# Three steps instead of two per converted weight slot, and a reordered opening, in a fused attention and two-FFN kernel

## The chip, the cores and the metric

The kernel runs on one core of one Trainium2 chip. The metric is the device time of one execution in microseconds (us), the median over several runs.

## What is computed

The reference chains three things; the shapes are those of the run.

- Causal attention over q, k, v of shape (2, 12, 448, 64): softmax(q k^T / 8 with a causal mask) v, reshaped to 896 tokens by 768.
- A dense FFN: `h = x @ w_in` (768 by 2048), `g = h * sigmoid(1.702 h)`, `x = g @ w_out` (2048 by 768).
- A second, routed FFN: of 8 experts each token goes to the one with the largest gate logit; `relu(x @ w1[e]) @ w2[e]` (768 by 1024, 1024 by 768), scaled by the gate's probability and a sigmoid of a second gate.

The weights of the dense FFN, w_in and w_out, arrive as 64-bit floats (the launch views them as int64), all else as 32-bit.

## The kernel before, in words

The program is written under a manual schedule: each engine executes its instructions in the order in which the Python code emits them, and waits only for the semaphores of the data it needs. So the order of emission is the order of each queue.

**Attention.** The 24 heads are worked in 12 pairs. Each pair has seven blocks of 64 queries (both heads stacked to 128 rows), taken in the order JO, so the stage is 84 numbered steps, s = 0 to 83, plus a drain of six. A step emits, in this order: the transposes of the probabilities of the step four earlier (`p_tr`, L405, and the copies L408 or L410), the scores and mask products of this step (`qk`, L374 and L375), the normalisation of the step before (`norm`, L395 to L397, the last mostly on POOL), at some steps the transposes of the next pair's q and k (`tr_qk`, L356, with the copies L361 and L365) and the products with v (`av`, L423), then this step's maximum and exponential (`soft`, L386 and L388), and last, at s % 7 equal to 3 or 6 from s = 7 on, one `pump`.

**Slot conversion.** [...] A `Stream` turns each 512 KB piece (128 by 512 numbers) into a slot: a high part in PE's rounded float format and a low part, the rest. There are 48 pieces: 24 of w_in, 8 of w_out's last 256 columns (`oB`), 16 of its first 512 (`oA`). The generator `work` (L222) does one piece, and `pump(n)` advances it by n steps, a step being what lies up to the next `yield`. Step A has two DVE operations (L226 and L228) and then `st.flush()`, which emits the DVE subtraction L235 of the piece before; step B has one DVE operation (L232) and the ACT copy L234, and registers this piece's subtraction as `late`. Then the generator ends, the piece counts as ready, its raw buffer is given back and the next load is emitted on SP's queue (L218). A piece takes two steps. `need(key)` forces steps until a piece is ready. Nineteen slots (ring A) and five raw buffers exist; where no slot is free, a pump does nothing.

**First layer.** 16 blocks f of 128 hidden units, six pieces kk each; `l1_mm` (L444) emits six products per kk into two PSUM tiles, of 512 and 384 columns. Even f take their two tiles from a pool of three (`sc`), odd f from a pool of four (`tp`). After each kk of f = 0 to 11 there is one step of the pump, after each kk of f = 12 to 14 there are two; at the last block of each group of four a slot is freed after each kk. Then the block's sigmoid (ACT, L547) and product (DVE, L548) run in four pieces and free the tiles.

**Second layer.** For t = 0 to 6, first part B (256 columns), then part A (512): 16 kk with three products each (L587). Its left factor is split by `gsplit` (ACT L516, DVE L519, four per t), up to four ahead. `y` is copied by ACT (L609), sent out, transposed (L627) and used for the gate (L639). Pump rates per kk are R2 in part B (0.1 to 0.3) and R3, 1.2, in part A. When the last piece is done, the loads of the experts' weights begin (`fill`).

**Experts.** Blocks of 128 tokens per expert, whose weights stream in, are split (L307 on ACT, L308 on DVE) and used (L897).

**Opening.** POOL makes the identity; DVE copies it to bf16 (L171) and clears `wz` (L456); eight warming products on `wz` run on PE (L459) into an unused tile; `load_pair(0)` issues q's two and k's two transfers on SP's queue (L339), and v's and the next pair's follow there. `tr_qk(0, "q")` transposes q, ACT scales it in two halves (L361), `tr_qk(0, "k")` follows with one ACT copy (L365), and the first scores can start.

Of the kernel before, what the change touches and what calls it, by code (L numbers as in the profile page):

```python
# [9 lines left out]
F32 = mybir.dt.float32  # L10
F32R = mybir.dt.float32r
BF16 = mybir.dt.bfloat16
# [3 lines left out]
AF = mybir.ActivationFunctionType  # L16
ALU = mybir.AluOpType
# [98 lines left out]
def kernel(ctx, tc, q, k, v, w_in, w_out, w_gate, w_og, w1, w2, out):  # L116
    nc = tc.nc
# [4 lines left out]
    CP = 112  # L122
# [33 lines left out]
    def pool(name, side="left", **kw):  # L156
        return tc.tile_pool(name=name, bufs=1, side=side, reuse_waits="tile", **kw)

    def opened(p):
        es = ExitStack()  # L160
        return es, es.enter_context(p)
# [4 lines left out]
    with tc.manual_schedule():  # L166

        ident = const.tile([128, 128], F32, name="ident")
        make_identity(nc, ident)
        identb = const.tile([128, 128], BF16, name="identb")  # L170
        nc.vector.tensor_copy(identb, ident)  # L171
        cmask = const.tile([128, QB], BF16, name="cmask")
        for h in range(2):
            make_causal_mask(nc, cmask[QB * h:QB * h + QB], mask_val=NEG)
# [35 lines left out]
        def raw_tile(where, shape, dt):  # L210
            if where == "raw":
                return raws.tile(shape, dt, name="raw", tag="raw", bufs=RAW)
            return ringA.tile(shape, dt, name="rawA", tag=f"slotA{where}")

        def add64(keys, src, two=False, ring="A"):
            def load(where):
                raw = raw_tile(where, [128, 512], I64)
                nc.sync.dma_start(raw.rearrange("p (a n) -> p a n", a=2) if two else raw, src)  # L218
                return raw

            def work(keys, raw):
                slot = st.slots[keys[0]] = ring_slot(keys[0])  # L222
                r = raw.bitcast(U32).rearrange("p (n two) -> p n two", two=2)
                w = raws.tile([128, 512], F32, name="w32", tag="w32", bufs=2)
                wu = w.bitcast(U32)
                nc.vector.tensor_scalar(wu, r[:, :, 1], 3, 0x3FFFFFF8,  # L226
                                        op0=ALU.logical_shift_left, op1=ALU.bitwise_and)
                nc.vector.scalar_tensor_tensor(wu, r[:, :, 1], 0xC0000000, wu,  # L228
                                               op0=ALU.bitwise_and, op1=ALU.bitwise_or)
                st.flush()  # L230
                yield
                nc.vector.scalar_tensor_tensor(wu, r[:, :, 0], 29, wu,  # L232
                                               op0=ALU.logical_shift_right, op1=ALU.bitwise_or)
                nc.scalar.copy(slot[:, 0], w)  # L234
                st.late = keys[0], lambda: nc.vector.tensor_sub(slot[:, 1], w, slot[:, 0].bitcast(F32))  # L235

            st.add(keys, ring, load, work)
# [3 lines left out]
        def ring_slot(key):  # L241
            ring, place = st.home[key]
            if ring == "A":
                return ringA.tile([128, 2, 512], F32R, name="slotA", tag=f"slotA{place}")
            return xr_p[0].tile([128, 2, 512], F32R, name="slotX", tag=f"slotX{place}")
# [69 lines left out]
        es_a, ap_ = opened(pool("attn", side="right"))  # L315
# [4 lines left out]
        NQ = S // QB  # L320
        KC = 128
        NKC = -(-S // KC)
        ld = {}
        qkT = {}
        P_t = {}
# [7 lines left out]
        def load_pair(i):  # L333
            b, hp = pairs[i]
            r = {}
            for nm, src in (("q", q), ("k", k)):
                t = ap_.tile([CP, NB, 2, D], F32, name=nm + "raw", tag=nm + "raw", bufs=2)
                for h in range(2):
                    nc.sync.dma_start(t[:, :, h, :], src[b, 2 * hp + h].rearrange("(c p) d -> p c d", p=CP))  # L339
                r[nm] = t  # L340
            ld.setdefault(i, {}).update(r)

        def load_v(i):
            b, hp = pairs[i]
            t = ap_.tile([KC, 2, NKC, D], F32, name="vraw", tag="vraw", bufs=3)
            full = S // KC
            for h in range(2):
                nc.sync.dma_start(t[:, h, 0:full], v[b, 2 * hp + h, 0:full * KC].rearrange("(c p) d -> p c d", p=KC))
            nc.sync.dma_start(t[0:S - full * KC, :, full], v[b, 2 * hp:2 * hp + 2, full * KC:S].rearrange("h p d -> p h d"))
            ld.setdefault(i, {})["v"] = t  # L350

        def tr_qk(i, nm):
            src = ld[i][nm]
            ps = pa.tile([128, 512], F32, name="ps_tr", tag="tp", bufs=TP)[:, 0:S].rearrange("p (c n) -> p c n", c=NB)
            for c in range(NB):
                nc.tensor.transpose(ps[:, c], src[:, c].rearrange("p h d -> p (h d)"), ident[:CP, :CP])  # L356
            if nm == "q":
                dst = qz[i % 2]
                for h in range(2):
                    r = slice(64 * h, 64 * h + 64)  # L360
                    nc.scalar.mul(dst[r, :, h], ps[r].rearrange("d c p -> d (c p)").rearrange("d (j p) -> d j p", j=NQ),  # L361
                                  0.125)
            else:
                dst = ap_.tile([128, S], F32, name="kT", tag="kT", bufs=2)
                nc.scalar.copy(dst.rearrange("d (c p) -> d c p", c=NB), ps)  # L365
            qkT[i, nm] = dst
# [32 lines left out]
        def p_tr(i, j):  # L399
            if j == JO[0]:  # L400
                pT[i] = ap_.tile([KC, 2, NQ + 5 * (NKC - 1), QB], F32, name="pT", tag="pT", bufs=2)
            nch = j // 2 + 1
# [11 lines left out]
        def av(i, c):  # L414
            b, hp = pairs[i]
            if c == 0:
                po[i] = pa.tile([128, S], F32, name="ps_o", tag="o", bufs=1)
            ps = po[i]
            vt = ld[i]["v"]
            t = pT[i]  # L420
            kn = min(KC, S - c * KC)
            for h in range(2):
                nc.tensor.matmul(ps[64 * h:64 * h + 64, c * KC:S], vt[:kn, h, c, :],  # L423
                                 t[:kn, h, 7 * c:5 * c + NQ], start=c == 0, stop=c == NKC - 1)
            if c < NKC - 1:
                return
            del ld[i], pT[i], po[i]
            dst = xhi[:, hp, b * S:(b + 1) * S]
            nc.scalar.copy(dst, ps)
            nc.vector.tensor_sub(xlo[:, hp, b * S:(b + 1) * S], ps, dst.bitcast(F32))  # L430
# [16 lines left out]
        early = 0  # L447
        steps = [(i, j) for i in range(NP) for j in JO]
        load_pair(0)
        load_v(0)  # L450
        load_pair(1)
        nc.gpsimd.memset(qz[0], 0.0)
        load_v(1)
        load_v(2)
        wz = ap_.tile([128, 512], BF16, name="wz")
        nc.vector.memset(wz, 0.0)  # L456
        wps = pa.tile([128, 512], F32, name="ps_w", tag="o", bufs=1)
        for i in range(WARM):
            nc.tensor.matmul(wps, wz[:, 0:128], wz, start=True, stop=True)  # L459
        tr_qk(0, "q")  # L460
        for j in range(0, NQ, 2):
            nc.gpsimd.memset(Pb[j][:, QB * (j + 1):], 0.0)
        nc.gpsimd.memset(qz[1], 0.0)
        tr_qk(0, "k")
        for s in range(len(steps) + LAG + AV_AT[-1]):
            if 0 <= s - LAG < len(steps):
                p_tr(*steps[s - LAG])
            if s < len(steps):
                i, j = steps[s]
                if s % NQ == 0 and i + 2 < NP:  # L470
                    load_pair(i + 2)
                qk(i, j)
            if 1 <= s <= len(steps):
                norm(*steps[s - 1])
            for c in "kq":
                if s < len(steps) and i + 1 < NP and s % NQ == TR_AT[c]:
                    tr_qk(i + 1, c)
            for c in range(NKC):
                u = s - LAG - (NQ - 1) - AV_AT[c]
                if u >= 0 and u % NQ == 0 and u // NQ < NP:  # L480
                    av(u // NQ, c)
                    if c == NKC - 1 and u // NQ + 3 < NP:
                        load_v(u // NQ + 3)
            soft()
            if s >= len(steps) + L1_PAST and early < KD - 1:
                l1_mm(0, early)
                early += 1
            if s % NQ in PUMP_AT and s >= PUMP_FROM and s < len(steps) + PUMP_PAST:
                st.pump(1)
# [70 lines left out]
        ps = ctx.enter_context(pool("ps", space=PSUM))  # L560
# [477 lines left out]
```

## Time and profile before

| what | value |
|---|---|
| median of three runs | 625.28 us (625.07 to 625.89) |
| the profiled execution: its own time | 625.63 us |
| span in the profile | 623.5 us |
| mean granted PE clock | 0.987 |
| PE busy | 590.3 us, 95% of the span |
| DVE busy | 463.9 us, 74% |
| ACT busy | 376.9 us, 60% |
| POOL busy | 106.7 us, 17% |

The profiled execution took 625.63 us, of which the span, from the first to the last recorded instruction, is 623.5 us; 2.1 us lie around it. An engine's busy time is the sum over its instructions. PE's products are pipelined and their ends are modelled, so a busy PE is not a PE at its peak. PEld is PE's weight load, which overlaps the products. By the timeline, attention lasts until about 125 us, the first layer until 252 us, part B of the second until about 302 us, part A until about 389 us, and the experts take the rest.

### The profile page before, as it was taken

The numbers are of one execution on the slowest core, as the hardware profiler recorded it, in microseconds if no ns is written. First come the engines' busy times: TensorE is split into PE (matmuls) and PEld (weight loads), VectorE is DVE, ScalarE is ACT, GpSimd is POOL, SyncE is SP. The second block draws the span as 40 slices with busy tenths as digits, with TensorE's granted clock in tenths as the row PEclk, the third lists the DMA queues.
The fourth block names the chain that finished last, engine by engine and source line by source line (L and its number), as shares of the span: only waits on it lengthen the run. The fifth ranks groups of instructions, "written<-read, shape, count | busy, mean of one in ns | idle before, by whom it ended". The sixth has DMA issues, their size and how long they took to land. (4 is left out here: it accounts for less than half of the span.)

```text
span 623.5 us, 10060 instructions
## 1 busy us (share of the span) xinstructions
PE 590.3 (95%) x3326; PEld 473.6 (76%) x3326; DVE 463.9 (74%) x942; ACT 376.9 (60%) x743; POOL 106.7 (17%) x225
## 2 busy tenths in 40 slices
PE   7999999899979999889999999989999999999995
PEld 4665665578868888879877777767888888888884
DVE  2788888757858483797633447789998898889886
ACT  4878878623232323455433234678888888888885
POOL 3333333310000000000001002231631111001110
PEclk8999999999979999999999999999999999999998
DMA  5856554216434241433571503359999999999940
GB/s 134 245 125 141 123 126 116 56 57 184 142 111 115 89 136 37 143 116 119 176 263 38 150 17 119 111 183 347 349 368 353 318 383 377 380 381 378 383 161 20
DMA packets 93146, 118.02 MB, mean 189 GB/s; under 512 B 40208, under 2 KB 53408, under 8 KB 93090
## 3 DMA queue, kind: packets, MB, share of 16 engines
q1 hardware_dynamic: 88562, 109.05, 54.7%
q0 software_dynamic: 2512, 5.54, 2.5%
q10 hardware_dynamic: 2016, 2.75, 1.2%
q8 instruction: 28, 0.46, 0.4%
q14 instruction: 28, 0.23, 0.1%
HBM read 114.10 MB, written 7.54 MB: 195 GB/s over the span
## 5 line engine op out<-in xcount | busy, mean ns | idle before, releaser
L587 PE MATMUL py<-slotA,gs 128*128 128x256 f32 (+1 forms) x609 | 112.5, 337 | 1.0 <-DVE gs L519 1.0
L444 PE MATMUL ph<-xhi,slotA 128*128 128x512 f32 (+1 forms) x384 | 97.7, 374 | 5.6 <-DVE g L548 5.6
L587 PEld LDWEIGHTS py<-slotA,gs 128*128 128x128 f32 x609 | 90.8, 190 | 13.6 <-issue 2.6
L444 PEld LDWEIGHTS ph<-xhi,slotA 128*128 128x128 f32 x384 | 70.8, 191 | 16.5 <-issue 6.1
L234 ACT CAST slotA<-w 128x512 fp32r<-128x512 f32 x45 | 27.9, 621 | 63.1 <-DVE w L232 61.4
L308 DVE TENSOR_TENSOR ent<-wraw,ent 128x1024 fp32r<-128x1024 f32 x48 | 57.9, 1221 | 5.8 <-ACT ent L307 5.8
L444 PE MATMUL ph<-xlo,slotA 128*128 128x512 f32 x192 | 56.1, 373 | 0.0
L374 PE MATMUL sc<-kT,qz 128*128 128x64 f32 (+6 forms) x168 | 53.2, 401 | 2.8 <-ACT kT L365 2.4
L388 ACT ACTIVATE P<-sc,nmax 128x64 f32<-128x64 f32 (+6 forms) x84 | 40.3, 479 | 24.5 <-DVE nmax L386 14.7
L548 DVE TENSOR_TENSOR g<-ph,g 128x256 f32<-128x256 f32 x64 | 23.6, 389 | 41.5 <-ACT g L547 41.5
L897 PE MATMUL ps_h<-ent,xh 128*128 128x512 f32 x192 | 54.0, 402 | 0.0
L307 ACT CAST ent<-wraw 128x1024 fp32r<-128x1024 f32 x48 | 49.9, 1053 | 0.0
L519 DVE TENSOR_TENSOR gs<-g,gs 128x512 fp32r<-128x512 f32 x56 | 37.5, 683 | 16.6 <-ACT gs L516 16.6
L397 POOL TENSOR_SCALAR P<-P,rc 128x64 f32<-128x64 f32 (+2 forms) x72 | 36.0, 500 | 69.6 <-DVE rc L396 43.5
L516 ACT CAST gs<-g 128x512 fp32r<-128x512 f32 x56 | 33.8, 618 | 16.3 <-PE py L587 10.6
L386 DVE TENSOR_REDUCE nmax<-sc 128x1 f32<-128x64 f32 (+6 forms) x84 | 34.4, 411 | 10.7 <-PE sc L375 10.7
L547 ACT ACTIVATE g<-ph 128x256 f32<-128x256 f32 x64 | 20.9, 355 | 33.5 <-PE ph L444 17.2
L897 PEld LDWEIGHTS ps_h<-ent,xh 128*128 128x128 f32 x192 | 35.0, 188 | 7.6 <-DVE ent L308 0.3
L308 DVE TENSOR_TENSOR ent<-wrb,ent 128x1024 fp32r<-128x1024 f32 x30 | 36.3, 1223 | 4.7 <-ACT ent L307 4.2
L444 PEld LDWEIGHTS ph<-xlo,slotA 128*128 128x128 f32 x192 | 35.8, 192 | 4.6
L405 PE MATMUL ps_pT<-ident,P 128*128 128x128 f32 x192 | 37.8, 289 | 1.1
L228 DVE SCALAR_TENSOR_TENSOR w<-raw,w 128x512 uint32<-128x512 uint32 x46 | 35.0, 762 | 1.6
(189 smaller groups left out, 1175.5 us busy)
## 6 DMA issues: line engine op xcount, KB each, us to landing
wraw<-in_moe_w_dram SPq DMA_DIRECT2D x66, 512.0 KB
wrb<-in_moe_w_dram SPq DMA_DIRECT2D x48, 512.0 KB
wr<-in_moe_w_dram SPq DMA_DIRECT2D x30, 512.0 KB
raw<-in_moe_w_in_dram SPq DMA_DIRECT2D x24, 512.0 KB
raw<-in_moe_w_out_dram SPq DMA_DIRECT2D x22, 512.0 KB
qraw<-in_q_dram SPq DMA_DIRECT2D x24, 112.0 KB
kraw<-in_k_dram SPq DMA_DIRECT2D x24, 112.0 KB
vraw<-in_v_dram SPq DMA_DIRECT2D x24, 96.0 KB
```

The lines of the kernel that those rows point to most:

```text
L228: nc.vector.scalar_tensor_tensor(wu, r[:, :, 1], 0xC0000000, wu, op0=ALU.bitwise_and, op1=ALU.bitwise_or)
L307: nc.scalar.copy(hi, raw)
L308: nc.vector.tensor_sub(lo, raw, hi.bitcast(F32))
L374: nc.tensor.matmul(sc[:, :n], qT[:, j].rearrange("d h p -> d (h p)"), kT[:, :n], start=True, stop=False)
L386: nc.vector.tensor_reduce(nm, sc[:, :n], axis=AX.X, op=ALU.max, negate=True)
L388: nc.scalar.activation(Pb[j][:, :n], sc[:, :n], AF.Exp, bias=nm, scale=1.0, accum_out=sm)
L397: eng[NORM_ENG[j]].tensor_scalar(Pb[j][:, :n], Pb[j][:, :n], rc, 1.0, op0=ALU.mult, op1=ALU.mult)
L405: nc.tensor.transpose(ps[:, c].rearrange("p h q -> p (h q)"), Pb[j][:, c * KC:(c + 1) * KC], ident)
L444: nc.tensor.matmul(p[:, 0:128 * nt], wt, xt[:, kk, 128 * t0:128 * (t0 + nt)], start=kk == 0 and n == 0, stop=kk == KD - 1 and n == 2)
L519: glate.append(lambda: nc.vector.tensor_sub(gs[:, 1], src, gs[:, 0].bitcast(F32)))
L587: nc.tensor.matmul(py[:, :n], gt[:, kk % 4], wt, start=kk == 0 and m == 0, stop=kk == KF - 1 and m == 2)
L897: nc.tensor.matmul(hps[hf], xh[:, k0 + n], wt[:, n], start=k0 + n == 0 and m == 0, stop=False)
```

## The change

The slot conversion gets a second `yield`, after the ACT copy L234, so a piece takes three steps: A, B, and a third, C, that emits no arithmetic and only registers the subtraction and ends the piece (with the release of the raw buffer and the next load). The numbers of pumps and their rates stay as they are. In the opening, `wz` is cleared ahead of the identity's bf16 copy, a one-column exponential on ACT is put ahead of the first loads, the first pair's k is issued on ACT's queue, and the second half of the first pair's q is scaled by DVE.

```diff
--- before.py
+++ after.py
@@ -168,7 +168,6 @@
         ident = const.tile([128, 128], F32, name="ident")
         make_identity(nc, ident)
         identb = const.tile([128, 128], BF16, name="identb")
-        nc.vector.tensor_copy(identb, ident)
         cmask = const.tile([128, QB], BF16, name="cmask")
         for h in range(2):
             make_causal_mask(nc, cmask[QB * h:QB * h + QB], mask_val=NEG)
@@ -232,6 +231,7 @@
                 nc.vector.scalar_tensor_tensor(wu, r[:, :, 0], 29, wu,
                                                op0=ALU.logical_shift_right, op1=ALU.bitwise_or)
                 nc.scalar.copy(slot[:, 0], w)
+                yield
                 st.late = keys[0], lambda: nc.vector.tensor_sub(slot[:, 1], w, slot[:, 0].bitcast(F32))
 
             st.add(keys, ring, load, work)
@@ -320,6 +320,11 @@
         NQ = S // QB
         KC = 128
         NKC = -(-S // KC)
+        wz = ap_.tile([128, 512], BF16, name="wz")
+        nc.vector.memset(wz, 0.0)
+        ez = ap_.tile([128, 1], F32, name="ez")
+        nc.scalar.activation(ez, wz[:, 0:1], AF.Exp)
+        nc.vector.tensor_copy(identb, ident)
         ld = {}
         qkT = {}
         P_t = {}
@@ -334,9 +339,10 @@
             b, hp = pairs[i]
             r = {}
             for nm, src in (("q", q), ("k", k)):
+                dma = nc.scalar if i == 0 and nm == "k" else nc.sync
                 t = ap_.tile([CP, NB, 2, D], F32, name=nm + "raw", tag=nm + "raw", bufs=2)
                 for h in range(2):
-                    nc.sync.dma_start(t[:, :, h, :], src[b, 2 * hp + h].rearrange("(c p) d -> p c d", p=CP))
+                    dma.dma_start(t[:, :, h, :], src[b, 2 * hp + h].rearrange("(c p) d -> p c d", p=CP))
                 r[nm] = t
             ld.setdefault(i, {}).update(r)
 
@@ -358,8 +364,11 @@
                 dst = qz[i % 2]
                 for h in range(2):
                     r = slice(64 * h, 64 * h + 64)
-                    nc.scalar.mul(dst[r, :, h], ps[r].rearrange("d c p -> d (c p)").rearrange("d (j p) -> d j p", j=NQ),
-                                  0.125)
+                    src_h = ps[r].rearrange("d c p -> d (c p)").rearrange("d (j p) -> d j p", j=NQ)
+                    if i == 0 and h:
+                        nc.vector.tensor_scalar(dst[r, :, h], src_h, 0.125, None, op0=ALU.mult)
+                    else:
+                        nc.scalar.mul(dst[r, :, h], src_h, 0.125)
             else:
                 dst = ap_.tile([128, S], F32, name="kT", tag="kT", bufs=2)
                 nc.scalar.copy(dst.rearrange("d (c p) -> d c p", c=NB), ps)
@@ -452,8 +461,6 @@
         nc.gpsimd.memset(qz[0], 0.0)
         load_v(1)
         load_v(2)
-        wz = ap_.tile([128, 512], BF16, name="wz")
-        nc.vector.memset(wz, 0.0)
         wps = pa.tile([128, 512], F32, name="ps_w", tag="o", bufs=1)
         for i in range(WARM):
             nc.tensor.matmul(wps, wz[:, 0:128], wz, start=True, stop=True)
```

## Rows read from the trace of the kernel before

**Rows 1.** Windows: length; busy us of PE, PEld, DVE, ACT, POOL; PE clock, DMA share, GB/s

```profile
260.00:280.00 20.00, 16.75 (x139) 15.77 (x138) 19.71 (x36) 10.29 (x22) 0.00 (x0) 1.00 0.39 119
...
500.00:520.00 20.00, 20.00 (x113) 17.14 (x113) 17.90 (x19) 17.20 (x23) 2.54 (x2) 1.00 1.05 384
```

**Rows 2.** Timeline of the opening (start us, us, instruction, idle before); one window

```profile
0.75 0.93 SPq L339 DMA_DIRECT2D qraw<-in_q_dram  x2
...
1.59 0.27 DVE L456 MEMSET wz<- 128x256 uint32 x1
...
1.72 1.02 SPq L339 DMA_DIRECT2D kraw<-in_k_dram  x2
...
6.05 0.95 PE L356 MATMUL ps_tr<-ident,kraw 112*128 112x112 f32 x4
...
6.34 1.28 ACT L361 ACT_TABLE_LOAD   x1 [6.34 <-PE ps_tr L356]
...
8.75 0.53 ACT L365 COPY kT<-ps_tr 128x448 f32<-128x448 f32 x1
...
9.43 0.41 PE L374 MATMUL sc<-kT,qz 128*128 128x64 f32 x2 [2.42 <-ACT kT L365]
...
11.00:11.50 0.50, 0.50 (x2) 0.34 (x2) 0.27 (x3) 0.42 (x1) 0.00 (x0) 0.50 0.35 78
```

**Rows 3.** Timeline of one attention pair

```profile
64.83 0.76 DVE L232 SCALAR_TENSOR_TENSOR w<-raw,w 128x512 uint32<-128x512 uint32 x1
...
66.23 0.59 POOL L397 TENSOR_SCALAR P<-P,rc 128x384 f32<-128x384 f32 x1 [1.18 <-DVE rc L396]
...
66.88 0.55 PE L405 MATMUL ps_pT<-ident,P 128*128 128x128 f32 x3
...
68.72 0.97 PE L423 MATMUL ps_o<-pT,vraw 128*64 128x448 f32 x4 [0.42 <-DVE pT L408]
...
69.18 0.41 DVE L226 TENSOR_SCALAR w<-raw 128x512 uint32<-128x512 uint32 x1
...
71.16 0.28 DVE L386 TENSOR_REDUCE nmax<-sc 128x1 f32<-128x128 f32 x1
```

**Rows 4.** First FFN layer: a group of the page, timelines of PE and DVE, one window

```profile
L444 PE MATMUL ph<-xhi,slotA 128*128 128x512 f32 (+1 forms) x384 | 97.7, 374 | 5.6 <-DVE g L548 5.6
...
156.29 0.98 PE L444 MATMUL ph<-xhi,slotA 128*128 128x512 f32 x4
...
157.53 0.99 PE L444 MATMUL ph<-xhi,slotA 128*128 128x512 f32 x4
...
175.76 0.66 PE L444 MATMUL ph<-xhi,slotA 128*128 128x384 f32 x1 [5.02 <-DVE g L548]
...
164.28 0.42 DVE L548 TENSOR_TENSOR g<-ph,g 128x256 f32<-128x256 f32 x1 [1.03 <-ACT g L547]
...
174.32 0.42 DVE L548 TENSOR_TENSOR g<-ph,g 128x256 f32<-128x256 f32 x1 [0.97 <-ACT g L547]
...
179.81 0.42 DVE L548 TENSOR_TENSOR g<-ph,g 128x256 f32<-128x256 f32 x1 [0.97 <-ACT g L547]
...
176.00:183.00 7.00, 7.00 (x24) 6.15 (x25) 3.99 (x9) 2.10 (x6) 0.00 (x0) 0.63 0.34 109
```

**Rows 5.** Second layer's B part: timelines of PE and ACT

```profile
251.99 4.71 PE L587 MATMUL py<-slotA,gs 128*128 128x256 f32 x38
...
257.67 3.62 PE L587 MATMUL py<-slotA,gs 128*128 128x256 f32 x28 [0.97 <-DVE gs L519]
...
276.74 0.62 ACT L234 CAST slotA<-w 128x512 fp32r<-128x512 f32 x1 [1.92 <-DVE w L232]
...
277.68 0.44 PE L627 MATMUL ps_yT<-ident,y 128*128 128x128 f32 x2 [1.81 <-ACT y L609]
...
291.38 0.38 PE L627 MATMUL ps_yT<-ident,y 128*128 128x128 f32 x2
...
297.88 0.38 PE L627 MATMUL ps_yT<-ident,y 128*128 128x128 f32 x2
```

## The prediction

> **What bounds the kernel now.** I read the windows of the whole span first, then the timeline of each stage that the change touches. PE is the engine in demand nearly everywhere, but not at an even cost: in 260 to 280 it is busy 16.75 of 20 us while DVE is busy 19.71 [rows 1], so there DVE sets the pace. In the experts PE shows 20.00, and the DMA share is 1.05 against 0.39 in the earlier window [rows 1]. DVE converts all 48 weight pieces, and the question of this change is in which stage it does so.
>
> Three places lose PE time that a different spread could return. In the opening PE waits 2.42 us for kT, and at 11.0 the granted clock is 0.50, the 1.2 GHz level [rows 2]; five such half-microsecond windows in a row show it, up to 13.5. In the first layer PE waits 5.6 us in all for the product L548, 5.02 of it at once before 175.76, and behind that the clock is 0.63 over 7 us [rows 4]. In part B it waits on DVE directly (0.97 us) and on an ACT copy (1.81 us) that stands behind a conversion copy, which waits 1.92 us for DVE [rows 5]. Attention is a tight mesh of DVE, ACT, POOL and PE, with one PE wait per pair on a DVE copy, 0.42 us [rows 3].
>
> **Where the steps go.** I counted the pumps by the loops of the program. Attention emits 23. Before, these are 11.5 pieces; after, 7 pieces and the steps A and B of an eighth. Before, blocks f = 1 to 4 convert three pieces each, then the 19 slots are full and pumps come to nothing. After, f = 1 to 11 convert two each, f = 12 four, f = 13 three, f = 14 none. At the end of the layer both versions stand at 37 pieces. In part B before does 21 steps (10.5 pieces), after 27 (9 pieces); part A starts with half a piece open before and two after. No `need` has to force a step in either, so weights are never late by emission.
>
> **Opening.** `wz` is cleared at 1.59, behind a copy that waits for POOL [rows 2]. Ahead of it all the memset can start when SP's first issue does, at 0.75, so the warming products and q's transposes come up to 0.84 us earlier. k's transposes at 6.05 show no wait for data [rows 2], so PE was the bound there. Now k's two issues stand on ACT behind the memset (to 1.02), the table load (1.28 us) and a one-column exponential (I take 0.2; between 0 and the 0.53 of the whole kT copy): they start at about 2.5 instead of 1.72, 0.8 later. SP's queue loses them, so v's and the next pair's loads issue 1.02 us earlier, needed by nobody yet. When k landed before isn't seen, only that it was by 6.05; so the transposes start between 5.2 (PE's bound) and 6.85. The table load and ACT's two halves, which held ACT from 6.34 to 8.75, leave the path: one half goes to DVE, idle then, the table is already loaded. From the start of k's transposes it is 0.95 + some 0.15 + 0.53 + 0.15 to the scores: 7.0 to 8.6 instead of 9.43. The gain is 0.8 to 2.4; I take 1.6. The half clock follows the 2.42 us of idle PE; the idle time is now in two shorter parts, and I take it that the clock stays up: of some 3 us at half speed at most 1.5 come back, I take 1.2. Opening: **+2.8**.
>
> The Trainium skill (Trainium Kernel Development and Optimization, Key Constraints) speaks against the second queue: it says that transfers issued from SP, ACT and POOL run on the same 16 DMA engines and interleave, and that another issuing engine saves only issue time. By that rule the sum below would be 4.3 instead of 6.7; no row of before can show it, since all loads stand on one queue there.
>
> **Attention.** Now A and B fall at step positions 3 and 6 of every pair. After, in turn: A at 3 and B at 6; C at 3 and A at 6; B at 3 and C at 6. Position 3 has cover: A holds DVE from 69.18 to 71.16 and no PE wait on DVE follows before the 0.42 us one of the next pair [rows 3]. Position 6 has none: behind B (0.76 us) the reciprocal for POOL's 66.23 is late, and PE's transposes at 66.88 start just as POOL ends [rows 3]. A there is 1.98 instead of 0.76, 1.2 us more, against which the 0.42 us wait further on goes, as that copy then has time: +0.75 taken, bounds 0 and 1.98. It happens in four pairs. C there removes B: the 0.42 us wait and some of the POOL wait, 0.6 taken, bounds 0 and 0.76, three times. Sum 4 × 0.75 − 3 × 0.6: **−1.2**.
>
> **First layer.** The pace of PE is 1.24 us per kk (156.29 to 157.53), 7.44 per block. DVE's pace is read from the first product of one block to that of the next: 10.04 with three pieces (164.28 to 174.32), 5.49 with one (to 179.81) [rows 4]. So a piece costs 2.275 and the rest of a block, its product chain with ACT, 3.215. Before, f = 1 to 4 fall behind by 2.60 each, 10.4 in all; PE waited 5.6, so its PSUM tiles give a slack of 4.8. Behind the long wait the clock of 0.63 costs 0.37 × 7 = 2.6. Before loses 8.2.
> After, a block with two pieces takes DVE 7.765, 0.325 over PE: eleven blocks make 3.6. Block 12 with four takes 12.3, 4.9 over: 8.5 behind. f = 14 takes its second tile from the pool of three, the one that f = 12's first products free; with the same slack PE waits 8.5 − 4.8 = 3.7 us there. Block 13's further 2.6 delays no tile (f = 15 is in the pool of four, freed by f = 11) and is made up in f = 14. I take it that the clock falls again: 2.42 us of idle was enough in the opening, 5.02 here [rows 2, 4]. So 6.3 comes back, net **+1.9**.
>
> **Second layer.** A t of part B lasts 6.50 us undisturbed (291.38 to 297.88); its 48 products at 4.71/38 = 0.124 make 5.95 in the first, which has no transposes. From 251.99, the transposes in the seventh would be due at 251.99 + 5.95 + 18 × 0.124 + 5 × 6.50 = 292.6 and come at 297.88 [rows 5]: 5.2 us lost. In the three saturated t's (14 steps) a step was half a piece, 1.14 us, and becomes a third, 0.76: 5.3 us less DVE work. The first wait of 0.97 stays, as the first t has A and B in both; of the rest I leave 0.7. **+3.5**, bounds 0 and 4.2. Part A begins with two pieces in five kk instead of half a piece; `gsplit` is up to four units ahead and hides it but for the ACT copy of y: −0.3, bounds 0 and −1.8 (the wait of 277.68). The experts' first loads are emitted four kk later, some 4 × 6 × 0.124 = 3.0 us; DMA's low share hides them, and 3.0 is their price without that cover. The third step itself has no arithmetic and costs nothing.
>
> The experts follow: their reloads are issued as pieces are split, so they move with what stands before. Sum: 2.8 − 1.2 + 1.9 + 3.5 − 0.3 = 6.7. Against the profiled execution, 625.63, that is 618.9; the median of the runs, 625.28, stands 0.35 lower: **618.6**.
>
> **Rivals.**
> *The clock holds at f = 14.* The wait of 3.7 is shorter than 5.02; against it stands the opening, where 2.42 was enough. 618.6 − 2.6 = 616.0. Chance 0.15.
> *No wait at f = 14.* The slack would have to be 3.7 larger, for instance because steps run ahead while DVE waits for PE in early blocks; the fit above speaks against it, since it leaves DVE behind from the first block. 618.6 − 6.3 = 612.3. Chance 0.10.
> *k lands late and the clock falls as before.* v's loads now stand directly behind q's on SP's queue and run beside k's, which start 0.8 later; from the point where k's transposes start at 6.85 or later the scores come at 8.6 at best, PE idles as long as before, and the opening brings 0.4: 618.6 + 2.4 = 621.0. That k shares engines with v is what the page of the Trainium skill named above would have. Against it: q, which is alone, is through earlier. Chance 0.13.
> *The change only moves the debt.* DVE's work is the same, and what blocks 1 to 4 no longer do, blocks 12 and 13 and part B must. If the layers gain nothing and attention neither, the opening is left: 625.3 − 2.8 = 622.5. Against it: the counts above. Chance 0.07.
> *Slower: A at position 6 pays in full.* Its place is the chain from DVE over POOL to PE's transposes. If four pairs each pay the whole 1.98, nothing is given back and C gains nothing, that is 7.9, and the three displaced ACT copies (0.62 each) on position 3's path add 1.9: the other terms make 7.9, so 625.3 − 7.9 + 9.8 = 627.2. It decides from 1.98 a pair on. For it: PE starts at 66.88 just as POOL ends. Against it: the wait of 0.42 must then vanish. Chance 0.05.
>
> **The numbers.** The forecast keeps 0.50. The range 612.7 to 622.2 takes in the bounds of the opening, of attention and of part B and the rivals at 616.0 and 621.0, and leaves out the clean layer, the slower case and part of the fourth. A measurement of this kernel tells 0.2%, 1.25 us, from no change; all cases but the last lie beyond it on the fast side, and a part of the fourth near it: faster 0.93, same 0.03, slower 0.04.
>
> **What would show it.** Right: the first scores near 7.8 and no half clock at 11; pair lengths that alternate in threes instead of repeating; no wait for L548 at f = 4 and 6, and one of 3 to 4 us at f = 14; part B's waits on DVE gone but the first. Wrong: the first layer still losing 8 us in any place, pairs all longer than before, or the experts' stage growing by what the earlier stages gave.

## The result, and the profile after

| | before | changed |
|---|---|---|
| median of four runs | 625.58 us (625.07 to 625.89) | 616.95 us (615.74 to 617.63) |
| profiled execution, its own time | 625.63 us | 617.25 us |
| span in the profile | 623.5 us | 615.1 us |
| mean granted PE clock | 0.987 | 0.994 |

The changed kernel takes 0.9861 of the time before (95% interval 0.9843 to 0.9879): 8.6 us less, where 6.7 were forecast. (A fourth run of the kernel before moves its median from 625.28 to 625.58.) The two traces give the place. Each row is the same instruction in both; the fourth column is how much earlier it comes in the changed kernel, and the last what was gained since the row above it.

| instruction | before, us | after, us | earlier by | gained here |
|---|---|---|---|---|
| first scores' mask product | 9.67 | 7.62 | 2.05 | +2.05 |
| same, first of pair 3 (of 12) | 26.57 | 25.36 | 1.21 | −0.84 |
| same, last of pair 12 | 120.63 | 117.99 | 2.64 | +1.43 |
| first product of part B | 251.99 | 247.64 | 4.35 | +1.71 |
| transposes of y in part B's seventh t | 297.88 | 289.78 | 8.10 | +3.75 |
| end of the span | 623.5 | 615.1 | 8.4 | +0.3 |

The opening in the timeline of PE, DVE, ACT and the queue on ACT (start us, us, instruction, idle before it and what ended that), to be held against [rows 2] ("..." marks rows left out, here and below):

```profile
0.75 1.28 ACT L326 ACT_TABLE_LOAD   x1 [0.75 <-PEq L1029]
...
0.88 0.27 DVE L324 MEMSET wz<- 128x256 uint32 x1 [0.88 <-PEq L1029]
...
1.19 0.96 ACTq L345 DMA_DIRECT2D kraw<-in_k_dram  x2
...
2.05 0.20 ACT L326 ACTIVATE ez<-wz 128x1 f32<-128x1 bf16 x1
...
5.54 0.98 PE L362 MATMUL ps_tr<-ident,kraw 112*128 112x112 f32 x4
...
6.34 0.63 DVE L369 TENSOR_SCALAR qz<-ps_tr 64x448 f32<-64x448 f32 x1 [4.76 <-ACT qz L371]
...
7.14 0.69 PE L383 MATMUL sc<-kT,qz 128*128 128x64 f32 x2 [0.62 <-ACT kT L374]
...
9.76 1.73 PE L383 MATMUL sc<-kT,qz 128*128 128x448 f32 x2
```

The scores start at 7.14 instead of 9.43, and PE's idle time ahead of them is 0.62 instead of 2.42. But the products that follow are slow: the two of 448 columns take 1.73, where later ones of this form take about 1.0. Pair 1 takes 8.48 us from mask product to mask product, before 7.34, so 1.1 of the 2.05 goes again.

In attention the first mask products of pairs 4, 5, 6 and 7 bound three pairs, and each has another length:

```profile
34.66 0.19 PE L384 MATMUL sc<-cmask,identb 128*128 128x64 bf16 x1
...
44.21 0.19 PE L384 MATMUL sc<-cmask,identb 128*128 128x64 bf16 x1
...
53.10 0.19 PE L384 MATMUL sc<-cmask,identb 128*128 128x64 bf16 x1
...
62.56 0.19 PE L384 MATMUL sc<-cmask,identb 128*128 128x64 bf16 x1
```

9.55 (the pair behind a step A at position 6), 8.89 (behind a C there), 9.46 (behind a B); before, every pair from the fourth on took 9.46.

The first layer, to be held against [rows 4]: the group of the page, PE's one wait, the first products of four blocks on DVE, one window.

```profile
L453 PE MATMUL ph<-xhi,slotA 128*128 128x512 f32 (+1 forms) x384 | 97.4, 373 | 4.1 <-DVE g L555 4.1
...
231.43 0.41 PE L453 MATMUL ph<-xhi,slotA 128*128 128x384 f32 x1 [4.14 <-DVE g L555]
...
209.80 0.42 DVE L555 TENSOR_TENSOR g<-ph,g 128x256 f32<-128x256 f32 x1 [1.03 <-ACT g L554]
...
217.62 0.42 DVE L555 TENSOR_TENSOR g<-ph,g 128x256 f32<-128x256 f32 x1 [1.03 <-ACT g L554]
...
229.98 0.42 DVE L555 TENSOR_TENSOR g<-ph,g 128x256 f32<-128x256 f32 x1 [1.02 <-ACT g L554]
...
231.00:235.00 4.00, 3.57 (x12) 3.16 (x13) 3.59 (x9) 0.77 (x3) 0.00 (x0) 0.65 0.22 84
```

The waits of blocks 4 and 6 are gone. A block of two pieces takes DVE 7.82, the one of four pieces (f = 12) 12.36, and f = 14 pays for it with 4.14; behind that wait the granted clock is 0.65 over 4 us, and by the pace of PE's products 1.5 us are lost there (before, 2.4 by the same measure).

Part B, to be held against [rows 5] and the first of [rows 1]: two y transposes and the one wait that is left, and the window.

```profile
253.33 3.62 PE L594 MATMUL py<-slotA,gs 128*128 128x256 f32 x28 [0.97 <-DVE gs L526]
...
283.28 0.38 PE L634 MATMUL ps_yT<-ident,y 128*128 128x128 f32 x2
...
289.78 0.38 PE L634 MATMUL ps_yT<-ident,y 128*128 128x128 f32 x2
```

```profile
260.00:280.00 20.00, 19.76 (x164) 18.52 (x164) 17.93 (x35) 11.90 (x24) 0.00 (x0) 1.00 0.30 92
```

PE is busy 19.76 of the 20 us, before 16.75, and DVE 17.93, before 19.71: here the two have changed places, and the saturated stretch is gone.

### The profile page after: what moved, and what is told of

Read it like the earlier page. It is cut to its first block, busy times and chain, and to the rows that moved or that the text cites. A ratio compares the mean times of both kernels' runs of the same rounds, so it can differ in the third digit from the quotient of the medians.

```text
span 615.1 us, 10056 instructions
## 1 busy us (share of the span) xinstructions
PE 589.6 (96%) x3326; PEld 473.7 (77%) x3326; DVE 462.5 (75%) x943; ACT 377.4 (61%) x743; POOL 106.0 (17%) x225
## 3 DMA queue, kind: packets, MB, share of 16 engines
q0 software_dynamic: 2512, 5.54, 2.5%
## 5 line engine op out<-in xcount | busy, mean ns | idle before, releaser
L414 PEld LDWEIGHTS ps_pT<-ident,P 128*128 128x128 f32 x192 | 21.2, 141 | 20.9 <-POOL P L406 17.2
L227 DVE SCALAR_TENSOR_TENSOR w<-raw,w 128x512 uint32<-128x512 uint32 x46 | 32.8, 714 | 1.6
```

Of the source, the lines that this page charges most:

```text
L414: nc.tensor.transpose(ps[:, c].rearrange("p h q -> p (h q)"), Pb[j][:, c * KC:(c + 1) * KC], ident)
```

## The experiments

Edits are against the changed kernel unless said otherwise; each ratio is to the kernel before, run on the same chip in turn. Theory and rivals stand in what was expected.

**The two halves of the change, each alone.**

```diff
                 nc.scalar.copy(slot[:, 0], w)
-                yield
```

> The opening's four edits alone, conversion in two steps as before. Theory (the parts add): the first scores come 2.0 us earlier as in the changed kernel, pair 0 is some 1.1 longer at the 1.2 GHz level, and 1.2 us are left and carried to the end: about 624.4 us against 625.6, first-layer waits for L548 of 5.6 us as before. Rival A (the opening's gain was lost in attention's mesh): within 0.3 us of before. Rival B (the low clock of pair 0 in the changed kernel was chance of that one execution): pair 0 is 7.3 us or less and the time 622.5 to 623.4.

Measured: 623.64 us (622.83 to 624.72, six runs), ratio 0.9963 (0.995 to 0.9976): 2.3 us by the ratio, more than the trace of the changed kernel showed of the opening (1.2) and less than the 2.8 of the forecast; the time lies between the theory's 624.4 and rival B's 623.4 and decides for neither. In the profile pair 1 takes 8.45, and the first layer has the waits of the kernel before, 0.63 and 5.01 for the product. The other half is the kernel before with nothing but the third step:

```diff
                 nc.scalar.copy(slot[:, 0], w)
+                yield
```

> The third step alone, opening as before. Theory (the parts add): attention +0.9, first layer +2.2, second layer +3.7, together 7 us faster: about 618.2 us; one wait of about 4.1 us for the product of block f = 12 at f = 14, none at f = 4 and 6. Rival (the two parts interact, the layers gain only because the opening shifted them against the loads): less than 5 us faster, 620.5 or more.

Measured: 619.62 us, ratio 0.9895 (0.9878 to 0.9912), 6.6 us less by the ratio, between the theory's 7 and the rival's 5. Pairs of 9.56, 8.90 and 9.46 and one wait of 4.46 at f = 14: the pair lengths and the one wait that the changed kernel shows belong to the `yield`. 2.3 + 6.6 = 8.9 against the 8.6 of the whole: the halves add, within the intervals.

**The wait at f = 14: pumps spread evenly over the layer.**

```diff
-    R1, R1B = 1, 2
+    R1, R1B = 1, 1
```

> The changed kernel with one step per kk also in blocks 12 to 14 (R1B 1 instead of 2): these blocks then convert two pieces each instead of four, three and none. Theory (the slack of 4.8 us and 0.325 us per block): block 12 ends 3.9 us behind, below the slack, so no wait at f = 14 and no fall of the clock; 4.1 + 1.5 us come back, one piece more (36 instead of 37 done) goes to the second layer and costs at most 1: 611.3 to 612.5 us. Rival (the debt moves on): part B, near DVE's limit, takes the piece as PE waits of 2.3 us or more and others follow: 614 us or more.

Measured: 613.8 us, ratio 0.9801 (0.9784 to 0.9819), between the theory's 612.5 and the rival's 614. PE's wait at f = 14 is gone, but a shorter one stands at the border to the second layer, with the half clock behind it. PE's timeline and a window of this run:

```profile
243.09 0.50 PE L594 MATMUL py<-slotA,gs 128*128 128x256 f32 x2 [1.63 <-ACT gs L523]
```

```profile
243.00:247.00 4.00, 3.69 (x19) 3.48 (x20) 3.48 (x8) 3.32 (x10) 0.00 (x0) 0.67 0.09 6
```

So the wait at f = 14 does come from the four pieces of block 12, and a spread without them moves part of the debt to the next consumer of DVE.

**k's issue on SP, as before.**

```diff
-                dma = nc.scalar if i == 0 and nm == "k" else nc.sync
+                dma = nc.sync
```

> The changed kernel with the first pair's k on SP's queue again, all else kept. Theory (the second queue saves issue time only, and k's transposes wait for q's): first scores within 0.4 us of the changed kernel's 7.14, time within 0.4 us of it. Rival A (the second queue carries the opening): scores about 1 us later, 1 us slower. Rival B (k beside v and q delays q): scores earlier than 7.0, faster by 0.2 or more.

Measured: 617.67 us, ratio 0.9864 (0.9846 to 0.9883) against 0.9861: the second queue is worth nothing that can be seen. k's transposes are at 5.58 here and at 5.54 in the changed kernel, both behind q's on PE.

```profile
4.59 0.95 PE L362 MATMUL ps_tr<-ident,qraw 112*128 112x112 f32 x4
5.58 0.98 PE L362 MATMUL ps_tr<-ident,kraw 112*128 112x112 f32 x4
```

That is how the rule of the Trainium skill cited in the prediction (Trainium Kernel Development and Optimization, Key Constraints) would have it: another issuing engine saves only issue time. The trace agrees as far as this goes, since here even the issue time is hidden behind q's transposes. But the 4.3 us that the prediction drew from the rule did not come: with k on SP's queue the ratio is the same, so the opening gains without the second queue.

**Position 6 or position 4.**

```diff
-    PUMP_AT = (3, 6)
+    PUMP_AT = (3, 4)
```

> The changed kernel with attention's pumps behind steps 3 and 4 of a pair instead of 3 and 6. Theory (only what stands at position 6 holds PE; 3 has cover and 4, ahead of the products with v, too): the pairs of 9.46 and 9.55 become 8.9 like those behind an empty position 6; seven or eight pairs gain 0.56 to 0.65, together 4.2 to 4.7 us: about 612.5 us on the chip where the changed kernel takes 616.9. Rival (DVE's load in the pair sets its length, wherever the steps stand): the mean pair stays near 9.3, time within 0.7 us of the changed kernel's. A second rival (position 4 delays the maximum of the next step as 6 did): pairs with B or A there 9.2 to 10, others 8.9.

Measured: 612.95 us, ratio 0.9795 (0.9779 to 0.9811): the expected time by luck, for another reason. The pairs became longer, as the rival said: 9.70 behind A at 4, 9.92 behind B, 8.90 behind C. But no block of the first layer waits at all, and part B starts at 242.44 instead of 247.64. The position 4 has one pump more in the drain of the attention, so one step more, a C, is done when the layer starts, and its blocks end on A. Two first products of the layer on DVE in this run:

```profile
161.04 0.42 DVE L555 TENSOR_TENSOR g<-ph,g 128x256 f32<-128x256 f32 x1 [0.65 <-ACT g L554]
...
168.48 0.42 DVE L555 TENSOR_TENSOR g<-ph,g 128x256 f32<-128x256 f32 x1 [0.64 <-ACT g L554]
```

They are 7.44 apart, PE's pace, and wait 0.64 for the sigmoid instead of 1.03. From this came a new theory, of the phase: it matters which step of a piece comes last in a block.

**Fewer and more warming products.**

```diff
-    WARM = 8
+    WARM = 0
```

> The changed kernel without the eight warming products on wz. Theory (in this opening they buy nothing: q's transposes wait for q until 4.6 us and pair 0 runs at the 1.2 GHz level up to 13.4 in any case): first scores at 7.1, pair 0 of 8.5, time within 0.4 us of the changed kernel. Rival (they bring the rise at 13.4 forward): the clock rises later, pair 0 and 1 are longer, 1 to 2 us slower.

Measured: 617.7 us, ratio 0.9876 (0.9858 to 0.9895), not to be told from the changed kernel. q's transposes start at 4.72, now waiting for the transfer, where they started at 4.69 behind eight products. With `WARM = 16`:

> The changed kernel with 16 warming products instead of eight: PE is busy with them to about 8.0 us instead of 4.7. Theory (a longer unbroken busy stretch does not raise the clock before 13 here): first scores 2.9 to 3.4 later, pair 0 shorter only by what lies behind the rise, 2 to 3 us slower than the changed kernel. Rival (the clock rises within the longer stretch and holds): transposes and pair 0 run at the 2.4 GHz level, pair 0 of 7 us or less, at most 1 us slower.

Measured: 616.56 us, ratio 0.9851 (0.9835 to 0.9867). PE's timeline of this run:

```profile
1.21 5.41 PE L466 MATMUL ps_w<-wz 128*128 128x512 bf16 x16 [1.21 <-DVE wz L324]
6.45 0.55 PE L362 MATMUL ps_tr<-ident,qraw 112*128 112x112 f32 x4
...
8.44 0.41 PE L383 MATMUL sc<-kT,qz 128*128 128x64 f32 x2 [1.06 <-DVE qz L369]
...
9.78 0.93 PE L383 MATMUL sc<-kT,qz 128*128 128x448 f32 x2
```

The transposes take 0.55 instead of 0.98, the same two products of 448 columns 0.93 instead of 1.73: PE is at its full pace, as the rival said. But the scores come at 8.44 instead of 7.14; pair 1 takes 6.30 and ends at 14.99, and the median is 0.4 under the changed kernel's, which the intervals don't tell from nothing. One thing that takes from earlier scores stands in some traces with eight products: PE then waits for the second pair's k to land. The line is from the run with one step more, further down, where PE was at full pace:

```profile
8.93 0.57 PE L362 MATMUL ps_tr<-ident,kraw 112*128 112x112 f32 x4 [1.32 <-DMA kraw<-in_k_dram]
```

With sixteen products these transposes come at 9.37, and there is no such wait.

**The phase, first by way of a whole version.** Two steps per piece in attention, behind positions 3 and 4, three from the first layer on, pumps even:

```diff
-    PUMP_AT = (3, 6)
+    PUMP_AT = (3, 4)
...
-    R1, R1B = 1, 2
+    R1, R1B = 1, 1
...
-                yield
+                if st.third:
+                    yield
...
+        st.third = True
```

The flag is cleared where the stream is made and set where attention's pools are closed.

> A version to beat both: two steps per piece in attention, behind steps 3 and 4 (11.5 pieces there, as before), three steps from the first layer on, and one step per kk in blocks 12 to 14 too. Theory: pairs of 8.9 (5 us less than before's), blocks 1 to 11 with two pieces, block 12 two, 13 one, 14 none, so 0.325 us behind per block and no wait for L548, no wait at the border to the second layer either; part B as in the changed kernel. 1.0 for the opening, 5.5 attention, 8 first layer, 3.7 part B: about 607.5 us. Rival (full two-step load behind 3 and 4 holds the pairs at 9.46): 612 or more.

Measured: 618.01 us, ratio 0.9878 (0.9861 to 0.9894), a miss by 10 us. The layer has no wait for the product, as expected, but each pair has a B at position 4, and from pair 4 on the pairs take 9.92 (one 10.17), as behind B in the run with position 4 above: 0.46 more than before in each, 4.9 in all from pair 3 to the last mask product, where 5.5 less were expected. PE's timeline shows the probabilities late there:

```profile
54.99 0.44 PE L416 MATMUL ps_pT<-ident,P 128*128 128x128 f32 x2 [0.48 <-POOL P L408]
```

This run has both phases in its first layer. Its blocks end on A until some pumps come to nothing behind 205 us; the blocks behind that end on C, with a B as the last work, as in the changed kernel. The first products on DVE:

```profile
195.33 0.42 DVE L558 TENSOR_TENSOR g<-ph,g 128x256 f32<-128x256 f32 x1 [0.65 <-ACT g L557]
202.77 0.42 DVE L558 TENSOR_TENSOR g<-ph,g 128x256 f32<-128x256 f32 x1 [0.64 <-ACT g L557]
...
218.05 0.42 DVE L558 TENSOR_TENSOR g<-ph,g 128x256 f32<-128x256 f32 x1 [1.05 <-ACT g L557]
...
225.88 0.42 DVE L558 TENSOR_TENSOR g<-ph,g 128x256 f32<-128x256 f32 x1 [1.02 <-ACT g L557]
```

They are 7.44 apart ahead of the change of phase and 7.83 behind it, with two pieces in a block both times.

**The phase alone.** One step more between attention and the first layer:

```diff
         es_a.close()
+        st.pump(1)
```

> The changed kernel with one more step of the pump between attention and the first layer, so that a block's six steps run B C A B C A instead of A B C A B C. Theory (phase): the block's last step is then A, all DVE, behind which the sigmoid stands ready; the 1.03 us in which DVE waits for the conversion copy and the sigmoid on ACT shrinks to what PE leaves, a block costs DVE 6.74 instead of 7.77 and keeps up with PE's 7.44; no wait for L555 at f = 14, no fall of the clock: 4.1 + 1.5 less, about 611.3 us. Rival (lead: what helped with pumps at 3 and 4 was the position in attention or the one step done earlier): a third of a piece is worth 0.8 us of DVE time, the wait shrinks from 4.1 to 3.3 or so, 615.5 or more.

Measured: 610.62 us (609.93 to 610.72), ratio 0.9751 (0.9735 to 0.9768), against 0.9861 without the step. No wait of PE in the whole first layer, though DVE's work is the same, and part B starts at 240.30. DVE has two of its first products with no wait ahead of them:

```profile
137.63 0.42 DVE L556 TENSOR_TENSOR g<-ph,g 128x256 f32<-128x256 f32 x1
...
144.34 0.42 DVE L556 TENSOR_TENSOR g<-ph,g 128x256 f32<-128x256 f32 x1
```

So in this phase a block of two pieces costs DVE 6.71, as expected, and no longer 7.8: less than PE's 7.44. A lead would not change that cost. With `st.pump(2)`:

> The changed kernel with two more steps there, so that a block runs C A B C A B. Theory (phase): the last step B has its ACT copy right ahead of the block's sigmoid as in the changed kernel, a block costs 7.77 again, block 12 ends as far behind; the wait at f = 14 stays at 3 to 4.5 us and the time within 1 us of the changed kernel's. Rival (lead): two steps done earlier are 1.5 us of DVE time, the wait shrinks to 2.5 or less and the time is below that of the run with one step more.

Measured: 618.43 us, ratio 0.9882 (0.9866 to 0.9899), 1.5 above the changed kernel where at most 1 was expected. PE waits twice:

```profile
211.10 0.41 PE L453 MATMUL ph<-xhi,slotA 128*128 128x384 f32 x1 [0.76 <-DVE g L556]
...
231.28 0.66 PE L453 MATMUL ph<-xhi,slotA 128*128 128x384 f32 x1 [5.07 <-DVE g L556]
```

Together that is 5.83, more than the changed kernel's 4.14 and than the 3 to 4.5 expected. The extra 1.7 comes from the start: the added steps are a C and an A, block 0's own step is then B, and its copy on ACT (129.09) stands ahead of the sigmoid's table load (129.73), so that block 0's first product comes 1.6 later, measured from PE's own products, than in the other two kernels. The later blocks cost 7.82 again, with a wait of 1.02 each. A lead of DVE at the start of the layer is thus not what helps: one step more helps, two do not. The end of a block shows why. Changed kernel, the timelines of DVE and of ACT, a block that ends on C, which has no arithmetic, so that B is its last work:

```profile
215.31 0.68 DVE L235 TENSOR_TENSOR slotA<-w,slotA 128x512 fp32r<-128x512 f32 x1
215.92 0.68 DVE L231 SCALAR_TENSOR_TENSOR w<-raw,w 128x512 uint32<-128x512 uint32 x1
217.62 0.42 DVE L555 TENSOR_TENSOR g<-ph,g 128x256 f32<-128x256 f32 x1 [1.03 <-ACT g L554]
```

```profile
216.69 0.62 ACT L233 CAST slotA<-w 128x512 fp32r<-128x512 f32 x1 [1.64 <-DVE w L231]
217.21 0.38 ACT L554 ACTIVATE g<-ph 128x256 f32<-128x256 f32 x1
```

With one step more, a block that ends on A, the same two views:

```profile
171.84 0.69 DVE L227 SCALAR_TENSOR_TENSOR w<-raw,w 128x512 uint32<-128x512 uint32 x1
172.45 0.69 DVE L235 TENSOR_TENSOR slotA<-w,slotA 128x512 fp32r<-128x512 f32 x1
173.78 0.42 DVE L556 TENSOR_TENSOR g<-ph,g 128x256 f32<-128x256 f32 x1 [0.64 <-ACT g L555]
```

```profile
171.50 0.62 ACT L233 CAST slotA<-w 128x512 fp32r<-128x512 f32 x1 [1.65 <-DVE w L231]
173.36 0.38 ACT L555 ACTIVATE g<-ph 128x256 f32<-128x256 f32 x1 [1.24 <-PE ph L453]
```

In the first, the copy of the last piece waits 1.64 on ACT for B, the sigmoid stands behind the copy in ACT's queue, and DVE waits for both: 0.62 + 0.38 and a little, 1.03. In the second, the copy runs beside DVE's next operations; when the sigmoid's turn comes ACT is idle, and waits 1.24 for PE. DVE's wait of 0.64 is then only PE's pace, and there is slack on both sides. In a layer of six steps per block and three steps per piece the phase, once set, stays the same from block to block, as long as every pump does its step.

**The parts that gained, together.** One step per pair in attention at position 3 alone, two steps per piece there, three from the first layer on, and 16 warming products (which had gained nothing that could be told):

```diff
-    PUMP_AT = (3, 6)
+    PUMP_AT = (3,)
...
-    WARM = 8
+    WARM = 16
...
-                yield
+                if st.third:
+                    yield
...
+        st.third = True
```

> A version to beat all: in attention two steps per piece and one pump per pair, behind step 3 (6 pieces instead of 7.7), three steps from the first layer on, whose blocks then run B C A B C A, and 16 warming products. Theory: all pairs 8.9 (4.4 us less than in the changed kernel), no wait in blocks 1 to 11; blocks 12 and 13 with four pieces each fall 3.8 behind apiece, under the slack of 4.8 where it counts, so no wait at f = 14; 5.6 less there; 0.4 for the opening: about 606.5 us. Rival (the missing pieces are late: f = 4 waits for its weights, or the border to the second layer takes back 2 us or more): 609 or more.

Measured: 606.25 us (605.99 to 606.87), ratio 0.9683 (0.9667 to 0.9699): faster than both kernels, by 3.2% and, taking the two ratios, by 1.8%. The pairs take 8.9 (the first row below to the second), from pair 3 to the last mask product attention takes 4.1 less than in the changed kernel, the first layer has no wait, as with one step more (6.3 less), and part B starts at 236.36 and has one wait. 4.1 + 6.3 = 10.4, against the 10.7 between the medians:

```profile
86.75 0.19 PE L386 MATMUL sc<-cmask,identb 128*128 128x64 bf16 x1
...
95.64 0.19 PE L386 MATMUL sc<-cmask,identb 128*128 128x64 bf16 x1
...
242.04 3.62 PE L597 MATMUL py<-slotA,gs 128*128 128x256 f32 x28 [0.78 <-DVE gs L529]
```

With `WARM = 8` in this version:

> The fastest version so far (606.25 us) with eight warming products again instead of 16. Theory (with eight, the clock of pair 0 falls out differently from execution to execution, first scores 1.3 earlier but pair 0 anywhere from 6.6 to 8.5; with 16 the clock is up when the scores start and pair 0 is 6.3): the median is 0.2 to 1 us above the version with 16, and the runs lie further apart, over a range of 1.5 us or more against 0.9. Rival (the 1.3 us that the shorter warming saves are kept): 605.0 to 605.8 us.

Measured: 606.05 us (605.66 to 607.08), ratio 0.9682 (0.9669 to 0.9695): neither; eight and sixteen can't be told apart.

## Why the prediction was right, and where it was not

The total was right and the side too: 616.95 lies inside the range, 1.65 below the forecast. That it came so close is in part luck. The two layers, which make most of the gain, came as worked out, but by the traces the opening brought 1.2 up to pair 3 instead of 2.8, and attention +1.4 instead of −1.2: two errors, 1.6 and 2.6, of opposite sign. Either alone would still have left the time inside the range. Point by point:

**Part B** (+3.5). Measured +3.75 in the two traces. A step of a third of a piece instead of half took DVE out of the bound (17.93 busy of 20 us instead of 19.71), and the first wait, 0.97, stayed as said.

**First layer** (+1.9). Measured +1.7 from the last mask product to part B, by the chain that was given: two pieces per block on DVE at 7.82 (7.765 was worked out), no wait at f = 4 and 6, one at f = 14 of 4.14 (3.7 worked out). Mis-sized was "I take it that the clock falls again", at 2.6: it fell, but 1.5 was lost, since the half-speed stretch was shorter; before's 2.6 was 2.4 by the same measure. What the working had not seen is that "the rest of a block", 3.215, is no constant: 1.03 of it is the wait for the copy of B and the sigmoid, which another phase takes away (6.71 per block with one step more). The two-piece block being "0.325 over PE" was thus true of the order of steps that the program happened to have. The rival of no wait at f = 14 was priced at 6.3, and the run that reached it with attention unchanged (one step more) shows that the price was sound: 610.62 against 616.95. Its mechanism, steps that run ahead, was not what did it, for two steps more brought nothing, and what changed was the cost of a block.

**Attention** (−1.2). Wrong in sign: +1.4. C at position 6 gives 0.56 (0.6 taken). The step that failed is "A there is 1.98 instead of 0.76, 1.2 us more, against which the 0.42 us wait further on goes": the pair behind an A there is only 0.09 longer, not 0.75. A itself holds DVE for 1.66 there (34.91 to 36.57), not 1.98. PE's transposes do wait, and the timeline of PE has that wait, 0.87 for POOL:

```profile
37.85 0.55 PE L414 MATMUL ps_pT<-ident,P 128*128 128x128 f32 x3 [0.87 <-POOL P L406]
```

That step interval of the pair (from one mask product to the next) is 1.88 instead of 1.10. But the one behind it is 1.83 instead of 2.32, and the one ahead of it 1.42 instead of 1.62: 0.78 paid, 0.69 given back. The working had let one later wait of 0.42 go against it, and the pair gave time back in two places; what had held the first of them, ahead of the products of 448 columns, isn't shown.

**Opening** (+2.8). The scores came 2.05 earlier, more than the 1.6 taken; the clock term, +1.2, was wrong in the profiled execution, where pair 1 was 1.1 longer than before, with products at half the later pace (1.73 for the two of 448 columns). Over the runs the opening is less short than in that one trace: the kernel with the opening alone gains 2.3. In the profiles of eight kernels with this opening, pair 1 took 8.48, 8.45, 8.16, 7.47, 7.05, 7.79, 6.62 and 8.12, and pair 2 began at 15.13 on average, against 17.01 in the one profile before: 1.9. So the opening is worth 1.9 to 2.3 on average instead of 2.8, and more or less in any one execution. The step that failed is "I take it that the clock stays up": the earlier scores make all of the gain, and pair 1, at 7.34 before and 7.77 on average after, gave none of the 1.2 (some of these pairs also hold the wait for the second pair's k). The chain there was wrong at two more steps: "they start at about 2.5", behind the table load and the exponential, was 1.19, for k's transfers were issued on ACT's queue while the table load ran from 0.75 to 2.03; and the two halves of q, which the working had side by side on DVE and ACT, ran one after the other (DVE's started at 6.34, having waited for ACT's). In the changed kernel neither is seen to have moved the scores: k's issue on SP gave the same time, and the scores waited for kT (0.62), not for q.

**Part A and the experts** (−0.3). From the seventh t on the kernel gains a further 0.3 by the two traces: no loss is seen there, and the experts moved with what stood before.

**The rivals.** "The change only moves the debt" and "A at position 6 pays in full" fell with the counts above. "k lands late" fell with the transposes at 5.54, and moving k back to SP's queue changed nothing. "The clock holds at f = 14" fell by the granted clock of 0.65.

## What to carry to other kernels

When background work is cut into steps among blocks of a loop, ask which step comes last ahead of the block's own chain and what it puts into the queue of the engine that opens that chain: one step of shift, with the same work, was worth 1.1% here, while two steps were worth nothing. A step that is late at one place of a tight mesh is priced by the next waits that it can use up, all of them, and not by the first. And the best version came from that shift and from giving the stage without slack less to do (one step per pair instead of two) once the later stages had room for it.

## What the runs showed of the hardware

- A DMA issue on ACT was not held by a table load of the same engine, nor by the activation that the program emits ahead of it: the load ran from 0.75 to 2.03, k's issue started at 1.19, and the first activation came at 2.05. So the order of emission is not the order of start between a queue's transfers and its engine's arithmetic here.
- The pace of PE in the first 14 us varies between executions whose code is the same up to there: the two products of 448 columns took 1.73 in the changed kernel and 0.93 with two steps more in front of the first layer, a change far behind the opening. In the changed kernel the granted clock reads 1.00 all along there, though the durations are nearly doubled: the windows of the opening, PE's clock the third number from the end. (In the trace before the column does show the low level, 0.50 [rows 2], and the same two products take 1.73 as well.)

```profile
8.00:10.00 2.00, 2.00 (x8) 1.42 (x8) 0.86 (x4) 0.68 (x3) 0.00 (x0) 1.00 0.65 145
10.00:12.00 2.00, 2.00 (x5) 0.90 (x5) 0.42 (x1) 0.77 (x3) 0.55 (x2) 1.00 0.60 137
```

So at the start of these traces the pace is better read from durations than from that column. Behind sixteen warming products both profiles of such a kernel had the full pace from q's transposes on, pair 1 taking 6.30 and 6.31. What sets the moment of the rise with eight stays open.
- The length of a wait did not tell whether the clock fell behind it. A wait of 1.63 on PE at the border of the layers was followed by a granted clock of 0.67 over 4 us (the run with even pumps), and one of 1.82 in part B by 0.50 (the opening alone, wait at 276.07). But the same wait in the kernel before, 1.81 at 277.68 [rows 5], was followed by 1.00, and so was the first of part B, 0.97, in the changed kernel. The window from 278 to 280 of the opening alone, then of the kernel before:

```profile
278.00:280.00 2.00, 2.00 (x11) 1.78 (x10) 1.97 (x4) 1.14 (x2) 0.00 (x0) 0.50 0.48 123
```

```profile
278.00:280.00 2.00, 2.00 (x20) 2.00 (x18) 2.00 (x4) 1.41 (x3) 0.00 (x0) 1.00 0.80 266
```
